# Second and third pair of a fused attention and mixer kernel: ScalarE's root, scaling and rounding queued behind its copies in PSUM, and the remainder rows taken in one visit

## The chip, the cores and the metric

One core of a Trainium2 chip runs the whole kernel. The metric is device time in microseconds (us); the kernel before takes 773.45 us as the median of three runs (773.4 to 773.78). PE is TensorE (matmuls), ACT is ScalarE, DVE is VectorE, POOL is GpSimd, SP is the engine that issues most DMAs. "Bank" below means one of the tiles in PSUM into which PE accumulates.

## The reference, cut to what matters

There are 8 batches of 576 rows, 8 heads of 64 columns, so 512 columns. Attention has no softmax: per head `kv = k^T v`, `out = q kv`, then each row of a head is divided by its root mean square and multiplied with a gain:

```
kv  = einsum('bhsd,bhse->bhde', k, v)
out = einsum('bhsd,bhde->bhse', q, kv)
x   = out / sqrt(mean(out*out, -1) + 1e-6) * g_norm        # (8, 576, 512)
h   = relu(x^T @ w_tok1) @ w_tok2                          # tokens: 576 -> 256 -> 576
u   = x + h^T
out = u + relu(u @ w_ch1) @ w_ch2                          # channels: 512 -> 1536 -> 512
```

All arrays are fp32; the weights arrive as 64-bit floats and are rounded to fp32 on the chip.

## The kernel before, in words

The batches are worked in four pairs (0 to 3). For each pair there is an attention stage (`attention`) that makes x in five tiles X[pair, 0..4] (tiles 0 to 3 hold 2 x 128 rows, tile 4 the 64 remainder rows of both batches), and a token mixing stage (`token_mixing`) that turns x into u. They overlap: while pair p is mixed, the attention of pair p+1 runs. After the fourth pair the channel part begins at about 186 us; it is a long run of block products and isn't touched here.

**An order written out by hand.** Nothing is scheduled by a planner. `play` (L1413) walks through lists of short names (`start`, `middle`, `steady`, `last`, L1474 to L1544) and calls the step of each name; every step's instructions go to their engine in just this order (`keep_in_program_order`), and each engine works its own queue strictly in order. `steady[0]` (L1488) mixes pair 1 beside the attention of pair 2, `steady[1]` (L1493) mixes pair 2 beside pair 3. A leading "-" takes the step from the attention of the pair that is being mixed. The names, with tile c and half or side t:

- `a{c}`: PE's attention products of tile c into two banks; `g`, `q`, `t`: gain on DVE (L495), square on ACT (L499), sum of squares on DVE (L523). `q` of the second bank follows `g` of that bank, and `g` of the first follows `q` of the first: DVE and ACT take turns with a bank.
- `m`, `r`, `i`: mean on DVE (L528), root on ACT (L533), reciprocal with one refinement on DVE (L537 to L542). `s`: ACT scales one half of a tile, head by head (8 instructions, L558). `d`: DVE scales the other half in one instruction (L567). `p21`: POOL does it (L571).
- `kv`, `e`: k^T v on PE and its eviction by ACT. `u{i}`: tok2 of row tile i on PE, with its eviction (a DVE add, L128, or, for the tiles in `seeds`, an ACT copy). `z{i}` (`seed`, L703): ACT copies x into a bank before PE accumulates on it.
- A digit n: the next n steps of `stream` (L1400), the rounding of the channel weights. Block n of 14 has "scale" on ACT (two instructions, L182 and L187, or four, L197 and L200), then "clamp" (L203), "shift" (L207) and "add" (L212, a custom instruction) on DVE. "shift" of block n brings "scale" of block n+1 with it. `f{n}` fetches block n by DMA into one of four staging buffers, which comes free when "add" of block n-4 is done. In all 43 steps; what is left is done in `last`.
- `b`, `l`, `lq`, `lr`: DMAs on SP; `x`: transposes on DVE (L781).

**The seven block products.** For pairs 1 and 2 (`fast`, L599) the first token product is not done row tile by row tile but with seven products of 2x2 blocks. Sums of blocks of w_tok1 are made once by POOL (`mix_tok1`); sums of blocks of x are made per pair by POOL (`t_sum`, names y1 to y4, 128x1024 each). y4 needs X[pair, 3] after both `s30` and `d31`. Four banks are used: a, y, b, d. The order on PE is p1 (a), p5 (b), p6 (y), the attention product a0 of the next pair, p3 (y), p7 (d), p2 (a), then the remainder and p4 (d). Two ACT instructions sit in the chain of PE:

```
        def copied(name, of):          # L656
            h_bank(name)
            copy(bank[name], bank[of])
        def p1():                      # L660
            product("a", a_block(0, 0), x_block(11), True)
            copied("y", "a")
        def p6():                      # L667
            product("y", tok_sum(2), h1[1])
            copied("d", "y")
```

p6 accumulates on the copy "y", so it waits for that copy. p3 overwrites "y", so it waits for the copy "d". p7 copies b and d into h1 (L674), and p4 accumulates on d after that. The remainder rows (64 per batch) are added to y and a in `ha` (`rem_first`, L691) before p4, and to b and d in `hb` (`rem_last`, L697) after it; each is followed by its relus on ACT (L131) and adds on DVE.

Of the kernel before, what the change touches and what calls it, by code (L numbers as in the profile page):

```python
# [20 lines left out]
def kernel(  # L21
# [33 lines left out]
    P = 128  # L55
# [5 lines left out]
    J, JJ, HF, Q = 4, 5, 64, 32  # L61
# [42 lines left out]
    w_tok1r = tokw.tile([P, DTOK], F32, name="w_tok1r")  # L104
# [11 lines left out]
    def do(f, *a, **kw):  # L116
        return lambda: f(*a, **kw)
# [9 lines left out]
    def tensor_add(o, a, b, op=ALU.add, engine=nc.vector):  # L127
        return keep(engine.tensor_tensor(out=o, in0=a, in1=b, op=op))  # L128

    def relu(o, a):  # L130
        keep(nc.scalar.activation(o, a, AF.Relu))  # L131
# [4 lines left out]
    def matmul(*a, **kw):  # L136
        keep(nc.tensor.matmul(*a, **kw))  # L137
# [112 lines left out]
    def get_tok2(t):  # L250
        return block(S, lambda raw: [(raw, words(moe_w_tok2)[ts(t, P)])], w_tok2[:, t])
# [132 lines left out]
    def x_of(pair, i):  # L384

        return X[pair, i // 2][:, i % 2]
# [212 lines left out]
    fast = (1, 2)  # L599
# [11 lines left out]
    def token_mixing(pair, seeds, aside=()):  # L611
        h1, acc = {}, {}
# [19 lines left out]
        bank = {}  # L632
# [49 lines left out]
        def p4():  # L682
            product("d", a_block(1, 1), room)

        def rem(t, names):
            for side in range(2):
                r = ds(side * HF, HF)
                matmul(bank[names[side]], lhsT=w_tok1r[r, ts(t, P)], rhs=x_of(pair, 8)[r],
                       start=False, stop=True, skip_group_check=True)

        def rem_first():  # L691
            rem(0, "ya")
            relu(h1[1][:, 0], bank["a"])
            tensor_add(h1[0][:, 0], bank["y"], h1[0][:, 0])
            relu(h1[0][:, 0], h1[0][:, 0])

        def rem_last():  # L697
            rem(1, "bd")
            relu(h1[1][:, 1], bank["d"])
            tensor_add(h1[0][:, 1], bank["b"], h1[0][:, 1])  # L700
            relu(h1[0][:, 1], h1[0][:, 1])

        def seed(i):  # L703

# [38 lines left out]
        steps = {f"h{s}{t}": do(tok1, s, t) for s in range(2) for t in range(NTOK)}  # L743
# [3 lines left out]
        if pair in fast:  # L747
            steps |= {f"y{n}": do(t_sum, n) for n in range(1, 5)}
            steps |= {"p1": p1, "p2": p2, "p3": p3, "p4": p4, "p5": p5, "p6": p6, "p7": p7}
            steps |= {"ha": rem_first, "hb": rem_last}  # L750
        return steps | {"hr": tok1_rem} | {f"u{i}": do(tok2, i) for i in range(9)}


    xg, xt, uT = {}, {}, {}
# [674 lines left out]
    tok2 = [get_tok2(t) for t in range(NTOK)]  # L1429
# [38 lines left out]
    def spread_g():  # L1468
# [5 lines left out]
    start = [  # L1474
# [12 lines left out]
    steady = [[  # L1487
# [12 lines left out]
    attentions += [attention(p, ((0, 1), (2, 4), (3,))) for p in range(1, B // 2)]  # L1500

    mixings = [token_mixing(p, (2, 3, 4, 5, 6) if p in fast else (2, 4, 6)) for p in range(B // 2 - 1)]
    mixings.append(token_mixing(B // 2 - 1, range(2, 9), (0, 1)))
    more = {f"w{n}{k}": f for n, b in enumerate(first_rows[:1] + tok1[1:] + tok2 + first_rows[1:]) for k, f in enumerate(b)}
    more |= {f"f{n}": b[0] for n, b in enumerate(channel)}
# [139 lines left out]
```

## Time and profile before

| | |
|---|---|
| median of 3 runs | 773.45 us |
| the profiled execution's own time | 773.52 us |
| its span, first to last instruction | 771.5 us |
| PE busy | 760.4 us (99%), clock granted 1.00 |
| DVE busy | 648.5 us (84%) |
| ACT busy | 287.5 us (37%) |
| POOL busy | 130.5 us (17%) |
| mixing of pair 1, from p1 on PE | 71.5 to 114.4 us |
| mixing of pair 2 | 115.4 to 155.0 us |
| token mixing of pair 3 | 154.9 to 186.5 us |
| channel part | 186.5 us to the end |

By stretch of the span, busy us of each engine:

| stretch, us | length | PE | DVE | ACT | POOL |
|---|---|---|---|---|---|
| 78 to 90 | 12 | 10.49 | 10.19 | 8.82 | 2.36 |
| 90 to 102 | 12 | 12.00 | 9.68 | 10.54 | 0.76 |
| 102 to 115 | 13 | 13.00 | 11.35 | 7.82 | 4.95 |
| 115 to 128 | 13 | 11.79 | 9.92 | 8.17 | 8.20 |
| 128 to 140 | 12 | 12.00 | 9.54 | 8.48 | 0.00 |
| 140 to 156 | 16 | 16.00 | 13.99 | 14.94 | 4.27 |
| 156 to 172 | 16 | 16.00 | 15.31 | 9.78 | 1.64 |

A line of the timeline gives the start, the time from there to the end of the last of the merged instructions, engine, source line, operation, output <- inputs, shape and count, and in brackets how long the engine was idle before and what ended that wait. Helpers record operations, so L137 is every matmul and L128 every tensor-tensor; the tile names tell them apart. The views merge buffers of one name: `w_ch` is also where the block sums `room` and `tok_sum` live, `ps_h` is any of the four banks of the seven products.

### The profile page before, as it was taken

Reading aid. Unit: us, or ns where it says so; the run is one execution under the profiler, and the core shown is the slowest. Engines: PE = TensorE matmul, PEld = TensorE weight load, DVE = VectorE, ACT = ScalarE, POOL = GpSimd, SP = SyncE. Lnnn points to the kernel's source line nnn. Section 1 sums busy time; section 2 is a strip of 40 time slices with the busy share of each in tenths; the row PEclk is TensorE's granted clock in tenths of the full one; section 3 lists DMA queues with packets and bytes.
Section 4 is the critical chain, followed back from the end, with each engine's and each line's share of the span. In section 5 each row is a group of like instructions: output and inputs, shape, how many; then the busy total and the mean of one; then the engine's idle time right before and its main releaser. Section 6 shows DMA issues by size and latency. Waiting matters only on the chain.

```text
span 771.5 us, 12763 instructions
## 1 busy us (share of the span) xinstructions
PE 760.4 (99%) x4686; PEld 612.5 (79%) x4686; DVE 648.5 (84%) x960; ACT 287.5 (37%) x579; POOL 130.5 (17%) x134
## 2 busy tenths in 40 slices
PE   9998999999999999999999999999999999999998
PEld 8654454545888888888888888888888888888887
DVE  4868787897776769999978889997998996798996
ACT  3655766864210233521144242223352224325221
POOL 1115133113410000002240001042000218000204
PEclk9999999999999999999999999999999999999999
DMA  9999996797699796599898577999659879855679
GB/s 354 375 370 373 357 353 215 249 365 263 242 283 344 264 291 195 164 270 203 222 231 258 150 221 225 255 185 269 197 152 284 175 220 207 208 145 158 155 192 120
DMA packets 137965, 188.28 MB, mean 244 GB/s; under 512 B 48688, under 2 KB 95792, under 8 KB 135856
## 3 DMA queue, kind: packets, MB, share of 16 engines
q1 hardware_dynamic: 102096, 168.59, 68.2%
q0 software_dynamic: 34848, 18.36, 15.9%
q8 instruction: 38, 0.62, 0.3%
q10 hardware_dynamic: 960, 0.52, 0.2%
q14 instruction: 23, 0.19, 0.1%
HBM read 138.28 MB, written 49.15 MB: 243 GB/s over the span
## 4 chain that ended last, share of the span: by engine, by line
PE 92%; DVE 4%; DMA 2%; ACT 1%; issue 0%; SPq 0%; DVEq 0%; ACTq 0%
PE ps_d L137 28%; PE ps_b L137 19%; PE ps_a L137 19%; PE ps_u L137 7%; PE ps_h L137 6%; PE ps_v L137 5%; PE ps_c L137 3%; PE ps_w L137 2%; PE ps_kv L137 2%; DMA raw<-in_moe_w_tok_dram 1%; PE ps_o L137 1%; DMA v_in<-in_k_dram 1%; DVE x L495 1%; DVE ms L523 1%; DVE w_ch L781 1%; ACT x L558 0%
## 5 line engine op out<-in xcount | busy, mean ns | idle before, releaser
L137 PE MATMUL ps_d<-ui,w 128*128 128x256 f32 x504 | 118.6, 379 | 0.0
L134 ACT COPY ps_d<-ps_a 128x768 f32<-128x768 f32 (+1 forms) x56 | 32.0, 572 | 199.9 <-PE ps_a L137 196.9
L137 PEld LDWEIGHTS ps_d<-ui,w 128*128 128x128 f32 x504 | 95.8, 190 | 13.0
L128 DVE TENSOR_TENSOR v<-v,v 128x1536 f32<-128x1536 f32 (+2 forms) x70 | 103.2, 1482 | 0.3
L137 PE MATMUL ps_b<-sv,w 128*128 128x256 f32 x324 | 78.9, 379 | 0.0
L137 PE MATMUL ps_a<-v,w 128*128 128x256 f32 x324 | 78.7, 379 | 0.0
L1367 POOL DMA_DIRECT2D out_dram<-us x24 | 26.8, 1834 | 291.8 <-ACT p L134 286.5
L137 PEld LDWEIGHTS ps_b<-sv,w 128*128 128x128 f32 x324 | 61.2, 190 | 8.9 <-issue 0.6
L137 PEld LDWEIGHTS ps_a<-v,w 128*128 128x128 f32 x324 | 61.6, 190 | 8.4
L137 PE MATMUL ps_u<-h,w_tok 128*128 128x512 f32 (+1 forms) x160 | 64.7, 599 | 0.0
L131 ACT ACTIVATE v<-v 128x768 f32<-128x768 f32 (+1 forms) x54 | 42.6, 822 | 55.1 <-DVE v L128 55.1
L137 PE MATMUL ps_d<-v,w 128*128 128x256 f32 x258 | 62.7, 379 | 0.0
L1367 POOL DMA_DIRECT2D out_dram<-r x40 | 41.3, 1919 | 102.0 <-ACT p L134 80.3
L137 PE MATMUL ps_d<-sv,w 128*128 128x256 f32 x228 | 55.4, 379 | 0.0
L137 PEld LDWEIGHTS ps_d<-v,w 128*128 128x128 f32 x258 | 48.9, 190 | 6.6
L137 PEld LDWEIGHTS ps_u<-h,w_tok 128*128 128x128 f32 (+1 forms) x160 | 25.6, 179 | 31.1 <-issue 27.0
L137 PEld LDWEIGHTS ps_d<-sv,w 128*128 128x128 f32 x228 | 43.3, 190 | 5.9
L137 PE MATMUL ps_a<-uT,w 128*128 128x256 f32 x192 | 46.7, 379 | 0.0
L137 PE MATMUL ps_b<-ui,w 128*128 128x256 f32 x168 | 40.8, 379 | 0.0
L137 PEld LDWEIGHTS ps_a<-uT,w 128*128 128x128 f32 x192 | 36.5, 190 | 5.0
L128 DVE TENSOR_TENSOR v<-ps_b,u 128x768 f32<-128x768 f32 x28 | 26.8, 956 | 15.6 <-PE ps_b L137 12.5
L134 ACT COPY u<-ps_d 128x256 f32<-128x256 f32 (+1 forms) x44 | 23.2, 528 | 43.4 <-PE ps_d L137 43.4
(198 smaller groups left out, 1358.0 us busy)
## 6 DMA issues: line engine op xcount, KB each, us to landing
w<-parts SPq DMA_DIRECT2D x168, 384.0 KB
w<-parts SPq DMA_DIRECT2D x56, 192.0 KB
uT<-blocks SPq DMA_DIRECT2D x36, 256.0 KB
k_in<-in_k_dram SPq DMA_DIRECT2D x8, 1024.0 KB
v_in<-in_v_dram SPq DMA_DIRECT2D x8, 1024.0 KB
qT<-in_q_dram SPq DMA_DIRECT2D x8, 1024.0 KB
out_dram<-x POOLq DMA_DIRECT2D x16, 512.0 KB, 6.4
raw<-in_moe_w_ch_dram SPq DMA_DIRECT2D x8, 768.0 KB
```

Of the source, the lines that this page charges most:

```text
L128: return keep(engine.tensor_tensor(out=o, in0=a, in1=b, op=op))
L131: keep(nc.scalar.activation(o, a, AF.Relu))
L134: keep(nc.scalar.copy(o, a))
L137: keep(nc.tensor.matmul(*a, **kw))
L495: keep(nc.vector.tensor_mul(x, bank[c, h], g_sb.to_broadcast([P, number(c), D])))
L523: keep(nc.vector.tensor_reduce(stats_of(c)[0][:, h], sq[c, h], axis=AX.X, op=ALU.add))
L781: keep(nc.vector.transpose(y[:, :, o, 2 * i:2 * i + 2].rearrange("p b n t -> p n b t"), x[:, ts(o, DH)].rearrange("p (n b t) -> p n b t", ...
L1367: keep(nc.gpsimd.dma_start(to, t()[ds(b * Q, Q), at].rearrange("p n l j -> p n (l j)"), accum_op=ALU.add))
```

## The change

In both steady lists the steps `r3` (root) and `s30` (scaling of X[pair, 3]) and the first rounding steps move behind the copies into the banks: `r3` from before `p1` to behind it, `s30` and the rounding from beside `p1` and `p5` to behind `p6`. `ha` and `hb` become one step `hr`, placed after `p4`: all the remainder matmuls, on y, a, b and d, then the relus and adds. Rounding steps are dealt out anew: pair 1's list has 15 instead of 14, pair 2's 14 as before, so one fewer is left for `last`.

```
-        def rem(t, names):
-            for side in range(2):
-                r = ds(side * HF, HF)
-                matmul(bank[names[side]], lhsT=w_tok1r[r, ts(t, P)], rhs=x_of(pair, 8)[r],
-                       start=False, stop=True, skip_group_check=True)
-
-        def rem_first():
-            rem(0, "ya")
+        def p_rem():
+            for t, names in enumerate(("ya", "bd")):
+                for side in range(2):
+                    r = ds(side * HF, HF)
+                    matmul(bank[names[side]], lhsT=w_tok1r[r, ts(t, P)], rhs=x_of(pair, 8)[r],
+                           start=False, stop=True, skip_group_check=True)
             relu(h1[1][:, 0], bank["a"])
-            tensor_add(h1[0][:, 0], bank["y"], h1[0][:, 0])
-            relu(h1[0][:, 0], h1[0][:, 0])
-
-        def rem_last():
-            rem(1, "bd")
+            for t, name in enumerate("yb"):
+                tensor_add(h1[0][:, t], bank[name], h1[0][:, t])
+                relu(h1[0][:, t], h1[0][:, t])
             relu(h1[1][:, 1], bank["d"])
-            tensor_add(h1[0][:, 1], bank["b"], h1[0][:, 1])
-            relu(h1[0][:, 1], h1[0][:, 1])
...
     steady = [[
-        "kv00 kv01 e00 e01 -d40 f3", "-u8 y2 y3 -v8 -a3 -q30 -g31 -q31 -g30 -t30 -t31 x01 -m3 -r3 -lq1",
-        "p1 -i3 -d31 -s30 1 l0 b00 1", "p5 1 f4", "p6", "a0 q00 g01 q01 g00 y4", "p3 t00 t01 b01 x10", "p7 1", "p2 1", "ha 1",
-        "p4 1", "hb z2 z3 f5 f6 1", "a1 q10 g11 q11 g10 lq0", "kv10 kv11 e10 e11 t10 t11 m0 r0", "u0 i0 1 1",
-        "u1 z4 d00 s01 l1 1", "u2 z5 1", "a2 q20 g21 q21 g20", "a4 q40 t20 g41 q41 t21 g40 lr0 lr1", "u3 z6 d11",
+        "kv00 kv01 e00 e01 -d40 f3", "-u8 y2 y3 -v8 -a3 -q30 -g31 -q31 -g30 -t30 -t31 x01 -m3 -lq1",
+        "p1 -r3 -i3 -d31 l0 b00", "p5 f4", "p6 -s30 1 1", "a0 q00 g01 q01 g00 y4", "p3 t00 t01 b01 x10", "p7 1", "p2 1 1",
+        "p4 1", "hr z2 z3 f5 f6 1", "a1 q10 g11 q11 g10 lq0", "kv10 kv11 e10 e11 t10 t11 m0 r0 1", "u0 i0 1 1",
+        "u1 z4 d00 s01 l1 1", "u2 z5 1", "a2 q20 g21 q21 g20", "a4 q40 t20 g41 q41 t21 g40 lr0 lr1", "u3 z6 d11 1",
         "u4 s10 t40 t41 m2 r2 f7 1", "u5 i2 1 d20 d21 P2 x11", "u6 f8", "u7 b10 b11"], [
-        "kv00 kv01 e00 e01 -d40 f9", "-u8 y2 y3 -v8 -a3 -q30 -g31 -q31 -g30 -t30 -t31 x20 -m3 -r3 -lq1",
-        "p1 -i3 -d31 -s30", "p5 1", "p6 1", "a0 q00 g01 q01 g00 y4", "p3 t00 t01 x21", "p7 1", "p2 f10", "ha 1", "p4 1", "hb z2 z3 1 1",
+        "kv00 kv01 e00 e01 -d40 f9", "-u8 y2 y3 -v8 -a3 -q30 -g31 -q31 -g30 -t30 -t31 x20 -m3 -lq1",
+        "p1 -r3 -i3 -d31", "p5", "p6 -s30 1 1", "a0 q00 g01 q01 g00 y4", "p3 t00 t01 x21", "p7 1", "p2 f10 1", "p4 1", "hr z2 z3 1 1",
         "a1 q10 g11 q11 g10", "kv10 kv11 e10 e11 t10 t11 m0 r0 b20 b21", "u0 f11 i0 1", "u1 z4 d00 s01 1", "u2 z5",
         "a2 q20 g21 q21 g20", "a4 q40 t20 g41 q41 t21 g40", "u3 z6 d11 1", "u4 s10 t40 t41 m2 r2 1",
         "u5 i2 d20 p21 1", "u6 1 f12", "u7 1", "a3 q30 g31 q31 g30", "u8 v8 t30 t31 m3 r3 f13"]]
```

In the order of instructions on each engine this gives, for ACT around p1 to p7: squares of a3, copy y, root, copy d, eight scalings, one "scale" of the rounding, squares of a0, copies of b and d into h1. After `hr` it gives: relu a, two relus of h1, relu d, seeds z2 and z3, one "scale" of the rounding, squares of a1, the evictions of kv, the root of the next group.

More of the change, by code (lines that the diff above doesn't have):

```diff
@@ L749, in token_mixing @@
             steps |= {"p1": p1, "p2": p2, "p3": p3, "p4": p4, "p5": p5, "p6": p6, "p7": p7}
-            steps |= {"ha": rem_first, "hb": rem_last}
-        return steps | {"hr": tok1_rem} | {f"u{i}": do(tok2, i) for i in range(9)}
+        return steps | {"hr": p_rem if pair in fast else tok1_rem} | {f"u{i}": do(tok2, i) for i in range(9)}
     xg, xt, uT = {}, {}, {}
```

## The prediction

> **What bounds the kernel now.** I read the waits of PE first, then the timelines of PE, ACT, DVE and POOL between 68 and 187 us. PE is busy in 99% of the span, and the waits of PE hold one entry of size after the start (columns: us in total, times, longest):
>
> ```profile
> PE ps_h L137 <- ACT ps_h L134: 4.4, 3, 1.7
> ```
>
> The timeline of PE shows the three places, all in the seven products; the bracket is the idle time. The lines that follow in pair 1 are p2, remainder, p4, remainder; the last is token mixing of pair 3:
>
> ```profile
> 76.93 1.95 PE L137 MATMUL ps_h<-h,w_ch 128*128 128x512 f32 x4 [1.72 <-ACT ps_h L134]
> 78.81 1.16 PE L137 MATMUL ps_o<-kvp,qT 64*64 64x64 f32 x64
> 81.49 1.98 PE L137 MATMUL ps_h<-x,w_ch 128*128 128x512 f32 x4 [1.51 <-ACT ps_h L134]
> ...
> 85.03 1.88 PE L137 MATMUL ps_h<-x,w_tok 128*128 128x512 f32 x4
> 86.83 1.13 PE L137 MATMUL ps_h<-x,w_tok1r 64*128 64x512 f32 x4
> 87.89 1.98 PE L137 MATMUL ps_h<-w_ch,w_tok 128*128 128x512 f32 x4
> 89.81 1.13 PE L137 MATMUL ps_h<-x,w_tok1r 64*128 64x512 f32 x4
> ...
> 120.33 1.96 PE L137 MATMUL ps_h<-h,w_ch 128*128 128x512 f32 x4 [1.21 <-ACT ps_h L134]
> ```
>
> From 186 us on PE waits once, 0.4 us, so what PE has lost or won by then should come through to the end. The question is only what the change does to PE before 186 us.
>
> **What it removes.** A product of four instructions follows another after 1.72 us (83.31 to 85.03). Pair 1: p5 starts at 73.33, so p6 could start at 75.05 instead of 76.93: 1.88 us. "y" can be copied as soon as p1 ends (73.50), and p6's other operand, y2 on POOL, is ready at 73.70. p3 could follow a0 after 1.09 (78.02; "d" copied from 77.03 to 77.61) instead of after 2.68: 1.59. Pair 2: p6 at 118.96 instead of 120.33: 1.37. The remainder in one visit: p2 to the end of the second remainder takes 90.87 - 85.03 = 5.84; p2 1.72, p4 1.82 and eight remainder instructions 1.92 (row at 42.35, to 44.27) make 5.46: 0.38 per pair. Sum 1.88 + 1.59 + 1.37 + 0.76 = 5.60 us. That would be the change if nothing else were late.
>
> **What comes late next, pair 1.** Here are the rows of POOL and DVE that decide it: y4, and the "add" of block 0.
>
> ```profile
> 79.48 2.36 POOL L128 TENSOR_TENSOR w_ch<-x,h 128x1024 f32<-128x1024 f32 x1 [1.89 <-ACT x L558]
> ```
> ```profile
> 80.19 2.46 DVE L212 CUSTOM_DVE_ANT_1 w_ch<-w_ch,raw 128x1536 uint16<-128x1536 uint16 x1 [1.71 <-ACT w_ch L182]
> ...
> 93.88 0.69 DVE L495 TENSOR_TENSOR x<-ps_o,g_sb 128x512 f32<-128x512 f32 x1 [0.75 <-ACT sq L499]
> ```
>
> The add waits for "scale" of block 1 (L182), takes 2.46 us where the next ones take 0.96, and ends 0.81 after POOL's y4: DVE stands while POOL works. After the change copy d sits before s30, so s30 runs from 77.55 to E = 79.57 (2.02, as now), y4 to 82.08, add to 82.89, g01 starts at 82.93. ACT's second square follows g01 after 0.78 (83.17 to 83.95 now): 83.71; then copies of b and d to 85.30. p4 must wait for that copy, and p4 is no longer behind a remainder but right after p2. PE, gaining 3.47, wants it at 83.28 and gets it at about 85.4: a new stall of 2.1.
>
> [...]
>
> Next, the queues behind `hr`. DVE goes g01, g00, two sums, four transposes, clamp, shift, add, clamp, then the add of y: 82.93 + 3.72 (83.17 to 86.89 now) + 0.58 + 0.55 + 0.88 + 0.48 = 89.14. Relus of h1 end at 91.1, relu d and the seeds z2 and z3 at 92.6. Now "scale" of block 3 stands before the squares of a1, which it did not: two instructions of 0.80. The first square starts at 94.16; it starts now in this line:
>
> ```profile
> 92.23 1.09 ACT L134 COPY ps_u<-x 128x512 f32<-128x512 f32 x2
> 93.26 1.07 ACT L499 ACTIVATE sq<-ps_o 128x512 f32<-128x512 f32 x2
> ...
> 104.76 0.61 ACT L134 COPY ps_u<-x 128x512 f32<-128x512 f32 x1
> ```
>
> So 0.90 later. DVE waits for it (g10, 93.88 now) for 3.3 us instead of 0.75, then has the "add" of block 2 (0.88) ahead of the eviction of u0, less a wait that goes: g21 of a2 at 102.92 (101.72 now, +1.20). ACT's squares of a2 and a4 follow DVE, and behind them is seed z6 (the last line above): 105.96 to 106.57 instead of 104.76. u6 on PE accumulates on z6. Now it starts at 106.51 and z6 is 1.1 ahead. After the change PE is there at 104.8 (85.4, p4 1.82, remainder 1.92, a1 1.09, kv 2.48, u0 to u2 5.35, a2 0.98, a4 0.58, three u of 1.72) and waits to 106.65. **Pair 1 gives +0.15: its gain is spent twice.**
>
> **Pair 2.** Behind z6 "scale" of block 5 (1.6) now stands ahead of s10 and root 2: the reciprocals come at 110.72 (107.93 now), the scaling of X[2, 2] ends at 113.48 (111.01), and POOL's y1, y2, y3 end at 116.04, 119.17 and 121.53 (113.57, 116.91, 119.23). PE needs y1 at 117.4 and y2 at 119.1: p6 at 119.25, a gain of 1.08. The mean m3 is one of the DVE forms that stand while POOL works (75.45, 0.60, ending with y3, where 119.31 took 0.13), so it ends at 121.55; root, copy d (122.27; p3 wants 122.22), s30 to E = 124.86, y4 to 127.37. "add" of block 5 needs no scale and is through before y4. ACT then has scale 6, two squares and the copies of b and d: 128.45; p4 wants 127.64 and starts at 128.55. `hr` ends at 132.29, 0.39 ahead of 132.68. Then again: relus to 133.98, relu d, z2 and z3 to 135.55, "scale" of block 8 of four instructions (2.42) ahead of the squares: 137.97 instead of 135.15. DVE stands 3.5 us. z6 ends at 148.66; u6, now at 148.32, wants 147.95 and starts at 148.75: **+0.43**.
>
> **Pair 3.** DVE is full there (15.31 of 16 us) and starts later: "scale" of block 9 and s10 ahead of root 2 bring the reciprocals to 153.65 (150.27), "add" of block 9 (1.13) has moved ahead of a3's gain, which comes at 158.85 (155.71). s30 of pair 3 ends at 165.4; now:
>
> ```profile
> 160.54 2.02 ACT L558 ACTIVATE x<-x,inv 128x64 f32<-128x64 f32 x8 [1.03 <-DVE inv L542]
> ```
> ```profile
> 154.90 14.00 PE L137 MATMUL ps_h<-x,w_tok 128*128 128x512 f32 x32
> ```
>
> Of these 32 instructions the 21st is the first to read it, at 154.90 + 20 x 0.43 = 163.5, 0.95 after it is ready. After the change PE is there at 163.95 and waits to 165.45: **+1.9 in all**. The remainder tile (d40, 166.6) is in time for 170.8. The sums on DVE end some 3 us later than now, at about 184 for PE's use at 188: hidden. DMA: block 9's fetch and the qT behind it on SP, issued at 129.49 and 130.42 now, come earlier, since "add" of block 5 is earlier; f6 and what stands behind it come 5 us later, for use 30 us on: nothing either way.
>
> **Sum.** 773.52 + 1.9 = 775.4 us against the profiled execution's own time; that one is 0.07 above the median, which is less than the rounding here.
>
> **Bounds.** From ACT's end to PE is 0.06 to 0.15. The add behind y4: 0.81 to 0.96. What the walk can miss most is the two waits of DVE for the squares (3.3 and 3.5 against 0.75 and 0.17 now). If each is shorter by 1, u6 costs nothing in either pair, p6 gains, and pair 3 does not wait: 773.0 or a little below. If DVE is 2 us later still in pair 3, its wait grows by as much: 777.4.
>
> **Rivals.**
> - **The later waits are not there; one stall is left** (faster). If rounding behind `hr` does not hold the squares, z6 comes in time, and pair 1 keeps 3.85 less the 2.1 at p4 = 1.75, pair 2 keeps 0.39 to 1.75: 773.52 - 2.1 to 3.5, about 770.8. For it: ACT is busy only 8.8 of 12 us there. Against: it is order, not load; the scale stands ahead of the squares in the queue. It decides where z6 in pair 1 ends before 105.
> - **All of it is won**: 773.52 - 5.60 = 767.9. For it: each of the three waits is PE's own, with PE on the chain before and after. Against: p4's wait needs y4 and the add to be over 2 us sooner than the rows allow.
> - **The change does not reach the time**: the gains are spent at p4 and u6 and pair 3 just escapes: 773.4 to 774.5. This differs from the forecast in one margin, s30 against PE in pair 3.
> - **DVE's backlog grows**: more waits in pair 3 or at the start of the channel part, 777 to 779. Against: channel sums have 4 us in hand.
>
> **How the numbers follow.** Forecast 0.42; not reached 0.26; one stall left 0.18; all won 0.06; backlog 0.08. What a measurement of this kernel can tell is about 0.2%, 1.55 us: 771.9 to 775.0. The forecast lies just above that, so a third of it counts as within: faster 0.23, within 0.38, slower 0.39. The range 770.2 to 778.0 leaves out the all-won case and the far ends.
>
> **What would show it.** Right: no wait for the copies "y" and "d" at p6 and p3; a wait of about 2 at p4 of pair 1 for ACT's copy into h1; a wait at the seventh tok2 product (u6) in one or both pairs; DVE idle over 2.5 us at g10 waiting for ACT's square; a wait in pair 3's tok1 for L558. Wrong: if u6 starts before 105.5 in pair 1, the queue behind `hr` was not what I take it for; if pair 3's tok1 runs through, 1.5 us fall away.

## The result, and the profile after

The changed kernel takes 776.76 us (median of 7 runs, 775.57 to 776.91), the kernel before on the same chip 773.55 (773.4 to 774.44). The ratio is 1.0035, with a 95% interval of 1.0023 to 1.0046: slower by about a third of a percent, which is 2.7 us by the ratio and 3.2 between the medians. The profiled execution took 776.9, with a span of 775.0. PE was idle for 11.1 us in the span before and for 13.6 in the one after.

The waits of PE after (us in total, times, longest) have three new entries behind 68 us, and the 4.4 us for the copies in PSUM are gone:

```profile
PE ps_h L137 <- ACT h L134: 3.6, 2, 2.8
PE ps_u L137 <- ACT ps_u L134: 1.8, 2, 1.0
PE ps_h L137 <- ACT x L558: 1.8, 1, 1.8
```

The timeline of PE after shows where. These are p6, a0 and p3 of pair 1, p2, p4 and the remainder; then u6 of pair 1, p6 of pair 2, its p4 and u6, and token mixing of pair 3:

```profile
73.86 1.98 PE L137 MATMUL ps_h<-h,w_ch 128*128 128x512 f32 x4
75.77 1.16 PE L137 MATMUL ps_o<-kvp,qT 64*64 64x64 f32 x64
76.93 1.98 PE L137 MATMUL ps_h<-x,w_ch 128*128 128x512 f32 x4
...
80.47 1.88 PE L137 MATMUL ps_h<-x,w_tok 128*128 128x512 f32 x4
85.16 2.83 PE L137 MATMUL ps_h<-w_ch,w_tok 128*128 128x512 f32 x4 [2.82 <-ACT h L134]
87.92 2.76 PE L137 MATMUL ps_h<-x,w_tok1r 64*128 64x512 f32 x8
...
107.53 3.70 PE L137 MATMUL ps_u<-h,w_tok 128*128 128x512 f32 x8 [1.02 <-ACT ps_u L134]
...
120.01 1.98 PE L137 MATMUL ps_h<-h,w_ch 128*128 128x512 f32 x4
...
129.27 1.96 PE L137 MATMUL ps_h<-w_ch,w_tok 128*128 128x512 f32 x4 [0.77 <-ACT h L134]
...
149.79 3.70 PE L137 MATMUL ps_u<-h,w_tok 128*128 128x512 f32 x8 [0.83 <-ACT ps_u L134]
...
167.05 5.42 PE L137 MATMUL ps_h<-x,w_tok 128*128 128x512 f32 x12 [1.81 <-ACT x L558]
```

p6 and p3 run straight through, as they should: three brackets of the profile before are gone. In their place there are five others, of 7.25 us in all. And one thing has no bracket: the four instructions of p4 took 2.83 to their end and the eight of the remainder 2.76, where the same shapes take 1.9 and 2.0 elsewhere. The busy time by stretch has the reason in its column PEclk, the third from the right, which is the granted clock, 1.00 at full speed (here the rows from 82 to 93 us; the columns are the stretch, its length, the busy us of PE, its weight loads, DVE, ACT and POOL, then PEclk, the DMA engines' busy share and GB/s):

```profile
82.00:85.20 3.20, 0.38 (x2) 0.07 (x1) 3.20 (x6) 1.75 (x4) 0.00 (x0) 1.00 1.02 418
85.20:87.90 2.70, 2.70 (x4) 0.74 (x4) 2.63 (x7) 1.43 (x2) 0.00 (x0) 0.67 1.07 370
87.90:90.60 2.70, 2.70 (x9) 1.03 (x8) 1.75 (x3) 0.60 (x1) 0.00 (x0) 0.70 1.05 364
90.60:93.00 2.40, 2.40 (x110) 2.32 (x110) 1.86 (x4) 2.19 (x5) 0.00 (x0) 1.00 0.89 292
```

Behind the stall the clock averages 0.67 and 0.70 over two rows. Rows of 0.1 us show that these are averages: the clock is 1.00 until 86.1, 0.50 from there to 89.5, and 1.00 again behind that. Half a clock for 3.4 us is 1.7 us of work lost.

The stall itself goes back to y4 and the "add" of block 0, which runs beside it as before; the gains of a0 come behind it, and through ACT's second square the copies of b and d:

```profile
79.58 2.37 POOL L128 TENSOR_TENSOR w_ch<-x,h 128x1024 f32<-128x1024 f32 x1 [1.86 <-ACT x L558]
```
```profile
80.28 2.48 DVE L212 CUSTOM_DVE_ANT_1 w_ch<-w_ch,raw 128x1536 uint16<-128x1536 uint16 x1 [1.70 <-ACT w_ch L182]
```

The queues behind `hr` read as forecast. On ACT and DVE after, the first square of a1, DVE's wait for it at g10, and seed z6:

```profile
95.09 1.06 ACT L499 ACTIVATE sq<-ps_o 128x512 f32<-128x512 f32 x2
...
106.87 0.61 ACT L134 COPY ps_u<-x 128x512 f32<-128x512 f32 x1
```
```profile
95.70 0.69 DVE L495 TENSOR_TENSOR x<-ps_o,g_sb 128x512 f32<-128x512 f32 x1 [3.15 <-ACT sq L499]
...
139.32 0.69 DVE L495 TENSOR_TENSOR x<-ps_o,g_sb 128x512 f32<-128x512 f32 x1 [3.42 <-ACT sq L499]
```

DVE stood 3.15 us in pair 1 and 3.42 in pair 2 for a square that stands behind a "scale" of the rounding; before it stood 0.75 and 0.17. The second of these is, before:

```profile
135.77 0.69 DVE L495 TENSOR_TENSOR x<-ps_o,g_sb 128x512 f32<-128x512 f32 x1 [0.17 <-ACT sq L499]
```

In pair 3 the scaling of X[3, 3] ran from 164.97 to 166.99 (160.54 to 162.56 before), and PE went on at 167.05. The channel part begins at 190.11 instead of 186.55: these 3.56 us are the loss, and behind that point nothing changes (the span is 3.5 longer). Its first line before, and after:

```profile
186.55 1.99 PE L137 MATMUL ps_v<-uT,w_ch 128*128 128x256 f32 x8
```
```profile
190.11 1.99 PE L137 MATMUL ps_v<-uT,w_ch 128*128 128x256 f32 x8
```

### The profile page after: what moved, and what is told of

Its sections match the earlier page's. It is cut to its first block, busy times and chain, and to the rows that moved or that the text cites. A ratio compares the mean times of both kernels' runs of the same rounds, so it can differ in the third digit from the quotient of the medians.

```text
span 775.0 us, 12764 instructions
## 1 busy us (share of the span) xinstructions
PE 761.4 (98%) x4686; PEld 611.8 (79%) x4686; DVE 648.5 (84%) x960; ACT 287.2 (37%) x579; POOL 131.5 (17%) x134
## 4 chain that ended last, share of the span: by engine, by line
PE 84%; DVE 7%; ACT 4%; DMA 2%; issue 2%; SPq 0%; DVEq 0%; ACTq 0%
PE ps_d L137 28%; PE ps_b L137 19%; PE ps_a L137 19%; PE ps_v L137 5%; PE ps_u L137 4%; PE ps_h L137 3%; PE ps_c L137 3%; PE ps_w L137 2%; ACT x L558 2%; DMA raw<-in_moe_w_tok_dram 1%; DVE ms L523 1%; DVE x L495 1%; PE ps_kv L137 1%; DMA v_in<-in_k_dram 1%; DVE x L567 1%
## 5 line engine op out<-in xcount | busy, mean ns | idle before, releaser
L137 PE MATMUL ps_h<-x,w_tok 128*128 128x512 f32 x80 | 37.1, 604 | 2.5 <-ACT x L558 1.8
```

## The experiments

**The theory**: moving the copies ahead is good by itself; the loss comes (1) from "scale" ahead of the squares of a1, behind `hr`, (2) from the add of block 0 that runs beside y4 and holds back p4, and (3) from the one rounding step more in pair 1, which shifts the stream, so that scales and adds stand ahead of squares, root and gain in pairs 2 and 3. **The rival**: the moved work is simply too much for DVE and ACT there, and any order of it ends in a wait. A second question is the clock: does it fall because PE stood still?

### Scale, gain, or both in another place; the copies alone

The first four were run together, beside the kernel before at 773.58 us (27 runs). Later groups ran on other chips; the kernel before took 773.51 to 773.65 us beside each of them, so that times are compared across groups here. The changed kernel was not run again beside them: its 776.76 is the one given above.

e1_scale_ahead_of_hr, both pairs:

```diff
-  "p4 1", "hr z2 z3 f5 f6 1", ...            "p4 1", "hr z2 z3 1 1",
+  "p4 1 1", "hr z2 z3 f5 f6", ...            "p4 1 1 1", "hr z2 z3",
```

> The changed kernel, with only the scale of the rounding that stood between the seeds and the squares of a1 moved ahead of the remainder (pair 1: one step, pair 2: two). If the queue behind the remainder is what costs (my theory), the square of a1 starts about 1.6 us sooner in pair 1 and 2 sooner in pair 2, DVE's wait for it falls below 2, neither u6 nor pair 3's tok1 waits (1.0, 0.8 and 1.8 less), while p4's wait of 2.8 in pair 1 and the lower clock behind it stay: 772.3 to 773.8 us. If the cost is the scaling of X[pair, 3] behind copy d and the stall at p4 with the clock that falls there (the rival), it stays at 775.5 to 777.

774.08 us (773.46 to 774.93), ratio 1.0004 [0.9995, 1.0014]: faster than the changed kernel, but a little above the 772.3 to 773.8 that the theory gave. The squares of a1 start at 92.69 instead of 95.09, u6 of pair 1 waits 0.44 instead of 1.02, and u6 of pair 2 not at all. p4 (2.81) still waits, as expected; tok1 of pair 3 (1.70) waits too, where the theory had it gone. So (1) is worth 2.7 us between the medians; in executions at a clock of 1.00 (below) it is 775.6 - 773.5 = 2.1.

e2_gain_ahead_of_add, pair 1:

```diff
-  "p6 -s30 1 1", "a0 q00 g01 q01 g00 y4",
+  "p6 -s30 1", "a0 q00 g01 q01 g00 y4 1",
```

> The changed kernel, with only the add of block 0 in pair 1 moved behind the gains of a0. If DVE's standing behind POOL's y4 makes p4 late, g01 starts near 78.7, the copy of d ends near 83 and p4's wait falls from 2.8 to about 0.9 us; the granted clock stays 1.00, so p4 and remainder take 3.7 instead of 5.5. The rival (stall and clock are the cost) then expects about 773 us or less. My theory expects the larger part of it to be lost again at u6, which waits for seed z6: 774 to 775.5, with u6's wait grown above 1 us in pair 1.

775.02 us (774.7 to 775.58), ratio 1.0017 [1.0008, 1.0026], within the theory's range. The timeline of PE in this kernel, p4 and u6 of pair 1:

```profile
83.08 1.96 PE L137 MATMUL ps_h<-w_ch,w_tok 128*128 128x512 f32 x4 [0.74 <-ACT h L134]
...
105.42 5.40 PE L137 MATMUL ps_u<-h,w_tok 128*128 128x512 f32 x8 [2.12 <-ACT ps_u L134]
```

p4's stall falls from 2.82 to 0.74, so all but this much of it was the add behind y4. But PE then comes to u6 earlier than the seed z6 and waits 2.12 there, and now these eight instructions take 5.40 instead of 3.70: the low clock has moved along with the longest stall. PE leaves the remainder 3.7 us ahead of the changed kernel (86.89 instead of 90.61: the shorter stall and the full clock) and leaves u6 only 0.4 ahead (110.75 instead of 111.16). In pair 2 p4 no longer waits (0.77 in the changed kernel), and from u6 of pair 2 on PE is 1.6 ahead, which is the 1.7 between the medians.

e3_both (the edits of e1_scale_ahead_of_hr and e2_gain_ahead_of_add):

> Both of the above. My theory: the waits at p4, u6 and pair 3's tok1 are all cut, 770 to 772 us, faster than the kernel before. The rival expects no more than the second alone brings, 773.

772.67 us (772.58 to 772.86), ratio 0.9984 [0.9975, 0.9993]; the theory's 770 to 772 is missed. p4 waits 0.75 in both pairs, u6 of pair 1 1.65, tok1 of pair 3 1.73. The two edits are worth 4.1 us between the medians, but not what the removal should bring; the wait in pair 3 is untouched by either.

e5_copies_alone: the kernel before, with the root behind copy "y" and scaling and rounding behind copy "d"; the remainder stays in two visits, the steps are 14 in pair 1:

```diff
-  ... x01 -m3 -r3 -lq1", "p1 -i3 -d31 -s30 1 l0 b00 1", "p5 1 f4", "p6",
+  ... x01 -m3 -lq1",     "p1 -r3 -i3 -d31 l0 b00",      "p5 f4",   "p6 -s30 1 1 1",
...
-  ... x20 -m3 -r3 -lq1", "p1 -i3 -d31 -s30", "p5 1", "p6 1",
+  ... x20 -m3 -lq1",     "p1 -r3 -i3 -d31",  "p5",   "p6 -s30 1 1",
```

> The kernel before, with only root, scaling and first rounding behind the copies; the remainder stays in two visits around p4, the rounding elsewhere as it was. My theory: the three waits for the copies go, p4 stands a remainder (1.06) later and waits less than 1.5 us, the scale ahead of the squares is not there, so u6 hardly waits: 770.5 to 772.5 us. The rival (the moved scaling is harmful by itself) expects 774 or more.

771.7 us (770.68 to 771.86), ratio 0.9967 [0.9955, 0.998]: faster. This half of the change, by itself, gains. PE has one wait of size left, at p4, longer than the 1.5 us that the theory allowed, and again with a low clock behind it (p4 2.67 to its end instead of 1.9):

```profile
86.01 2.67 PE L137 MATMUL ps_h<-w_ch,w_tok 128*128 128x512 f32 x4 [2.34 <-ACT h L134]
```

No wait at u6, none in pair 3. So the three waits of the copies can be had without the two late ones.

### One step less, the remainder alone, and the parts put together

The next four were run together, beside the kernel before at 773.51 us (21 runs).

e8_one_step_less: the changed kernel, one digit taken out of pair 1.

```diff
-  "u3 z6 d11 1",
+  "u3 z6 d11",
```

> The changed kernel with one rounding step taken out of pair 1 (the one behind u3, so that it is taken later), nothing else. Theory (the step too many is what shifts the stream, puts the scales of blocks 8 and 9 ahead of squares and root, and the add of block 9 ahead of the gain of a3): p4's 2.8 and u6's 1.0 in pair 1 stay, u6 of pair 2 and L558 of pair 3 no longer wait (0.8 and 1.8): 773.5 to 774.8. Rival (pair 2 and 3 are late because pair 1 was, or because of the one visit): waits as in the changed kernel, 775.5 to 777.

772.55 us (771.47 to 774.13), ratio 0.9985 [0.9976, 0.9994]. One digit is worth 4.2 us between the medians. p4 (2.61) and u6 of pair 1 (1.02) wait as in the changed kernel; all the waits of pairs 2 and 3 are gone, that of p4 in pair 2 among them. The first square of a1 in pair 2 comes at 135.02 (138.72 in the changed kernel), the scaling of X[3, 3] at 160.43 (164.97; 160.54 before):

```profile
135.02 1.08 ACT L499 ACTIVATE sq<-ps_o 128x512 f32<-128x512 f32 x2
...
160.43 2.02 ACT L558 ACTIVATE x<-x,inv 128x64 f32<-128x64 f32 x8 [1.03 <-DVE inv L542]
```

It went below what either theory gave: by its brackets the three waits are 3.4 us, by the starts of the instructions 4.2 (190.11 to 185.89 at the channel part), and the 0.77 at p4 of pair 2 had not been counted. This settles (3): what the forecast had as "scale of block 5", "of block 8" and "add of block 9" ahead of their neighbours is one step too many, and not the late pair 1, which is as late here (u6 starts at 107.64, and at 107.53 in the changed kernel).

e4_remainder_alone: the changed kernel's single visit with the copies, root, scaling and rounding where they were (the edit is against the kernel before).

```diff
-  "p7 1", "p2 1", "ha 1", "p4 1", "hb z2 z3 f5 f6 1",
+  "p7 1", "p2 1 1", "p4 1", "hr z2 z3 f5 f6 1",
...
-  "p7 1", "p2 f10", "ha 1", "p4 1", "hb z2 z3 1 1",
+  "p7 1", "p2 f10 1", "p4 1", "hr z2 z3 1 1",
```

> The other half of the change alone: the remainder of both token tiles in one visit of PE, with the copies y and d, the root and the scaling in the order of before, and as many rounding steps in pair 1 as before (14). Theory (the visit in one is cheap, the loss comes from the extra rounding step and from the stall at p4): p4 wants PE at about 86.7 and its copy is there at 85.5, so no wait at p4; the rounding steps have the phase of before, so no scale stands ahead of the squares of a1, no wait over 0.5 at u6, none at L558 in pair 3. The waits of 1.7, 1.5 and 1.2 for the copies stay. Time 772.5 to 773.6. Rival (the one visit itself throws VectorE back, because both additions and four relus now come behind the last product): VectorE waits over 2.5 us for the first square of a1 here too, u6 or tok1 of pair 3 waits over 1 us: 774.5 to 776.

772.99 us (772.68 to 773.92), ratio 0.9992 [0.9983, 1.0001]: 0.5 us, within what can be told from no change. p4 does not wait, nor u6, nor pair 3; VectorE waits 1.24 and 0.65 for the first squares, not over 2.5. The single visit is harmless; whether its 0.38 per pair is there, the time alone cannot tell. In this profile PE came to p6 1.0 us earlier than in the one of before and waited 3.11 for copy "y"; p4 is at 87.11.

e6_copies_gain_ahead: e5_copies_alone with the gain of a0 ahead of the add.

```diff
-  "p6 -s30 1 1 1", "a0 q00 g01 q01 g00 y4",
+  "p6 -s30 1", "a0 q00 g01 q01 g00 y4 1 1",
```

> The copies moved alone, with the remainder in two visits as before, and in pair 1 the gain of a0 ahead of the rounding's add. Theory (the 2.34 us at p4 and the low clock behind it are what was left of the loss in the kernel with the copies alone, and they come from the add behind y4): p4's wait is under 0.3, the granted clock stays at 1.00 from 80 to 95 us, and the time falls from 771.7 to 768.5 to 770. Rival (VectorE's work is only put off, and PE waits for it at u6 or in tok1 of pair 3 by about as much): 771 to 772.

769.85 us (769.62 to 770.14), ratio 0.9951 [0.9939, 0.9964]. p4 runs through and the clock is 1.00. Two waits come in its place, 0.45 at u0 for a relu and 1.08 at u6 for seed z6: the rival is there too, with 1.5 of the 2.3 us. That the time still falls by 1.9 about fits: 2.34 of waiting and 1.7 of slow clock go, 1.5 of waiting come, which makes 2.5; by the start of the channel part in the two profiles it is 2.2 (182.75 instead of 184.95).

e7_all_phase_of_before: the changed kernel with the gain ahead of the add and 14 steps in pair 1.

```diff
-  "p6 -s30 1 1", "a0 q00 g01 q01 g00 y4", ... "kv10 ... m0 r0 1", ... "u3 z6 d11 1",
+  "p6 -s30 1", "a0 q00 g01 q01 g00 y4 1 1", ... "kv10 ... m0 r0", ... "u3 z6 d11",
```

> The whole change, with the gain of a0 ahead of the add and with 14 rounding steps in pair 1 instead of 15, so that from pair 2 on the stream of steps stands as it did before. Theory: p4 waits 0.7 as in the kernel with the gain ahead, the two scales no longer stand ahead of the squares, u6 waits under 0.7 in pair 1 and not in pair 2, L558 not at all: 768.5 to 770.5, that is 2 to 4 below the kernel with scale and gain both moved (772.67). Rival (the phase does not matter, the load of VectorE does): u6 and L558 wait 1.6 and 1.7 as there, 772 to 773.

769.03 us (768.89 to 769.06), ratio 0.994 [0.9926, 0.9954]: the best version, 7.7 us below the changed kernel with the same instructions; only u6's wait is above the 0.7 that was expected. All that PE waits for between 68 and 186 us:

```profile
82.96 1.96 PE L137 MATMUL ps_h<-w_ch,w_tok 128*128 128x512 f32 x4 [0.74 <-ACT h L134]
103.54 3.70 PE L137 MATMUL ps_u<-h,w_tok 128*128 128x512 f32 x8 [0.88 <-ACT ps_u L134]
```

The rival "any order ends in a wait of the same size" has fallen. Of the 5.60 us that the removal was worth in the forecast, 4.5 are here.

e10_seed_earlier: e7_all_phase_of_before with the seed z6 of pair 1 ahead of the squares of a2. (Run with e9_no_idle_at_p4, beside 773.52, 9 runs.)

```diff
-  "u2 z5 1", ... "u3 z6 d11",
+  "u2 z5 z6 1", ... "u3 d11",
```

> The kernel with the whole change, the gain ahead and the phase of before (769.03), with the seed z6 of pair 1 put ahead of the squares of a2. Theory (u6's wait of 0.88 is only the seed behind the squares in ScalarE's queue): u6 of pair 1 does not wait, 768.2 to 768.7. Rival (the seed's bank comes free late or VectorE's gain of a2, 0.6 later, makes the evictions late): a wait of 0.5 or more at u5 to u7, 768.9 to 769.8.

769.12 us (768.71 to 769.42), ratio 0.994 [0.9927, 0.9952]: nothing gained over 769.03, though u6 does not wait any more. PE has a new wait of 0.75 at p4 of pair 2 instead. Neither theory had the place: the 0.88 at u6 go, and nearly as much is waited one pair later.

### Does PE's clock fall because PE stands still?

e9_no_idle_at_p4: the changed kernel with six products that nobody reads between p2 and p4 of pair 1.

```diff
+    def warm():
+        o = ps["kv"].tile([P, DM], F32, name="ps_w", tag="kv")
+        for _ in range(6):
+            matmul(o, lhsT=ones, rhs=w_tok2[:, 0, :DM], start=True, stop=True)
+
+    more["jw"] = warm
...
-  "p7 1", "p2 1 1",
+  "p7 1", "p2 1 1 jw",
```

> The changed kernel with six products of 128x512 that nobody reads between p2 and p4 of pair 1 (6 x 0.43 = 2.6 us by the rows of tok2), so that TensorE is busy through the stall of 2.8; p4 still starts when its copy is there. Theory (the missed 1.7 us are the granted clock, which falls because TensorE stood still): p4's wait is under 0.5, p4 starts at 85.2 as in the changed kernel, the clock stays at 1.00 from 85 to 91 us, p4 and the remainder take 1.8 and 1.9, and the times, which lay at 775.6 with a mean clock of 1.000 and at 776.9 with 0.998, all lie at 775.3 to 775.8. Rival (the clock falls for another reason in that stretch, such as what the other engines draw): the clock falls here too, in most executions, and the median stays at 776.5 to 777.

779.41 us (779.25 to 779.62), ratio 1.0073 [1.006, 1.0087]. The size was wrong: each product is two instructions, so the six took 5.2 us and not 2.6, and they waited 1.75 for a square of ACT before they began; p4 started at 89.31 instead of 85.16. As a measurement of the question it says one thing: with PE idle for 1.75 at a stretch, and then busy, the clock stayed at 1.00, and the mean clock was 0.999 or 1.000 in all five executions. p4 and the remainder took 1.88 and 1.99.

e11_idle_cut_short and e12_one_step_less_idle_cut: one such product instead of six, in the changed kernel and in e8_one_step_less (beside 773.65, 15 runs).

> The changed kernel with one product of 128x512 that nobody reads between p2 and p4 of pair 1: two instructions, 0.86 us by the rows of e9_no_idle_at_p4, where they started at 84.06. They end at about 84.95, ahead of 85.16, where p4 of the changed kernel gets its copy: p4 should start at the same time as there, but TensorE stands 1.75 us at a stretch instead of 2.82. Theory (the clock falls because TensorE stands too long): the clock stays at 1.00 from 85 to 91 us in every execution (mean 0.999 or 1.000), p4 and the remainder take 1.9 and 2.0 instead of 2.76 and 2.69, and the times lie at 775.3 to 776.0, all together. Rival (the clock falls for another reason in that stretch): most executions at 0.998 and 776.7 to 777, as in the changed kernel.

775.73 us (775.42 to 776.9), ratio 1.0027 [1.0016, 1.0039].

> The kernel with one step less in pair 1 (e8_one_step_less: times at 771.5, 772.6 and 774.0 with mean clocks of 1.000, 0.998 and 0.995), with the same one product between p2 and p4. Theory: all executions at 771.3 to 772.0, clock 0.999 or more. Rival: the levels of 772.6 and 774.0 are still there.

771.59 us (771.35 to 772.96), ratio 0.9976 [0.9967, 0.9986].

The executions sort by their mean granted clock. Times in us:

| kernel | PE idle at a stretch at p4 | clock 0.999 or 1.000 | clock 0.998 or less |
|---|---|---|---|
| changed | 2.82 | 3 of 7: 775.57 to 775.83 | 4: 776.76 to 776.91 |
| changed, e11_idle_cut_short | 1.75 | 5 of 7: 775.42 to 775.75 | 2: 776.73, 776.9 |
| e8_one_step_less | 2.61 | 3 of 11: 771.47 to 771.64 | 6: 772.5 to 772.82; 2 at 0.995: 773.98, 774.13 |
| e12_one_step_less_idle_cut | 1.76 | 7 of 9: 771.35 to 771.74 | 2: 772.85, 772.96 |
| e1_scale_ahead_of_hr | 2.81 | 3 of 11: 773.46 to 773.57 | 8: 773.88 to 774.93 |
| e2_gain_ahead_of_add | 0.74 (2.12 at u6) | 5 of 11: 774.7 to 774.94 | 6: 775.02 to 775.58 |
| e5_copies_alone | 2.34 | 2 of 5: 770.68, 770.84 | 3: 771.7 to 771.86 |
| e3_both, e7_all_phase_of_before | 0.75, 0.74 (1.65, 0.88 at u6) | 16 of 16 | none |

The mean does not say where in an execution the clock fell; only a profile does, and each kernel has one. In the changed kernel, e8, e11 and e12 an execution with a low clock is 1.0 to 1.4 us longer between the medians (2.5 at 0.995), in e1, e2 and e5 0.5 to 1.1. With the idle time cut to 1.75 it comes in 4 of 16 executions instead of 12 of 18, p4 itself starting as before. So it is rarer behind the shorter stall, as the theory says; but it did not go away, as the theory said. The profile of e11_idle_cut_short is one in which it came, that of e12_one_step_less_idle_cut one in which it did not; the lines are the extra product and p4 of pair 1:

```profile
83.98 1.13 PE L137 MATMUL ps_w<-w_tok,ones 128*128 128x512 f32 x2 [1.75 <-ACT sq L499]
85.04 3.65 PE L137 MATMUL ps_h<-w_ch,w_tok 128*128 128x512 f32 x4
```
```profile
84.11 1.12 PE L137 MATMUL ps_w<-w_tok,ones 128*128 128x512 f32 x2 [1.76 <-ACT sq L499]
85.16 1.96 PE L137 MATMUL ps_h<-w_ch,w_tok 128*128 128x512 f32 x4
```

The same instructions after the same wait take 3.65 us in the one and 1.96 in the other. What decides between the two executions stays open.

The two executions also give the price of a fall. e12_one_step_less_idle_cut and e8_one_step_less have the same pair 1 up to u6 but for the one product; p4 starts at 85.16 and 85.27. Without a fall the squares of a1 start at 93.84 and u6 at 106.26 after a wait of 1.40; with one, at 95.21 and 107.64 after 1.02. So of the 1.7 us that PE loses, some 0.4 are taken up by a shorter wait at u6, and 1.4 are left.

## Why the prediction was right, and where its size was off

The forecast was 775.4 us and the result 776.76. Its mechanism held step by step: every sign that it named as right is in the profile. One term was mis-sized, the work behind the new stall.

- **The removed waits.** p6 and p3 of pair 1 and p6 of pair 2 wait for no copy. e5_copies_alone shows that this is worth something: 1.9 us net of a new 2.3 us stall, and 3.7 with that stall gone (e6_copies_gain_ahead), of the 4.84 (1.88 + 1.59 + 1.37) that the forecast had for the copies.
- **p4 of pair 1.** Forecast: start at 85.4 after a wait of 2.1. Measured: 85.16 after 2.82; PE was there 0.9 earlier (p1 at 70.20 and not 71.51, since 1.1 us of idle time ahead of it, at ps_r with no releaser, is in the profile of before and not in this one). That is not the change: in the profiles of the experiments, two of them built on the kernel before, this idle time is at most 0.25 us. It made the stall longer and left p4's start where it was, since the copies of b and d set it, as the forecast said. The row of the add was right: it ended at 82.76, 0.81 behind y4 as before; the 0.96 at the upper end of the forecast's bounds is in neither profile.
- **The term that was mis-sized.** p4 and the remainder were priced at 1.82 and 1.92, from rows at a clock of 1.00. They took 2.76 (85.16 to 87.92) and 2.69 (87.92 to 90.61): 1.71 us more, with the clock at 0.50 for 3.4 us. The step that failed is the price of work *behind* a new stall. In the three executions with the clock at 1.000 or 0.999 the time was 775.57 to 775.83, 0.2 to 0.4 from the forecast.
- **The queue behind `hr`.** Forecast from p4's start on: squares of a1 at 94.16, DVE idle 3.3, z6 at 105.96, u6 of pair 1 at 106.65. Measured: 95.09, 3.15, 106.87 and 107.53, so the starts are some 0.9 later. Without a fall of the clock they are 0.3 to 0.4 earlier than forecast (93.84, 105.60 and 106.26 in e12_one_step_less_idle_cut, DVE idle 3.21), so the walk was right here and the clock is the difference. e1_scale_ahead_of_hr shows that the scale's place is the cause of the queue: the squares come 2.4 earlier there.
- **Pair 2.** y1 to y3 end at 116.87, 119.95 and 122.27 (forecast 116.04, 119.17, 121.53), p6 at 120.01 (119.25), p4 at 129.27 (128.55), DVE idle 3.42 (3.5), u6 at 149.79 (148.75): the same shape, 0.7 to 1.0 later.
- **Pair 3.** Forecast a wait of 1.5 for the scaling, to 165.45; measured 1.81, to 167.05. This is 1.6 later, where u6 of pair 2 was 1.0 later: some 0.5 were added on DVE, between the reciprocals (154.75, forecast 153.65) and the gain of a3 (160.40, forecast 158.85). The forecast gave pair 2 and 3 as the places where the gain is lost, to blocks 5, 8 and 9 standing one place further ahead. e8_one_step_less confirms this as one cause, and prices it at 4.2 us: one digit in one list.
- **The rivals.** "One stall left", 770.8, needs z6 of pair 1 to end before 105; it ended at 107.48. The 8.8 of 12 us that spoke for it are those of 78 to 90 us; behind the remainder, from 90 to 102, ACT was busy for 10.54 of 12. It is not this kernel; e7_all_phase_of_before and e6_copies_gain_ahead are near what it described, with the order changed. "DVE's backlog grows" was right in the small: pair 3's wait was 0.3 longer, and no new one came behind it.

## What to carry to other kernels

In a kernel whose order is written by hand, a step added early in a shared stream (here one rounding step of 14) shifts every later one by a place; look two stages on for what now stands ahead of a square, a root or a gain. An instruction moved out of the path of one wait has to be followed to the next place where PE meets the same queue: p4, u6 and pair 3 each took back a part here. And in this kernel the price of a stall of 1.75 us or more on PE was its length and, in many executions, 1.7 us of slower work behind it, less what a following wait took up (0.4 at u6).

## What the runs showed of the hardware

The granted clock of PE fell at stalls of 3.11 us (e4_remainder_alone), 2.82 (the changed kernel), 2.61 (e8_one_step_less), 2.34 (e5_copies_alone), 2.12 (e2_gain_ahead_of_add: eight instructions in 5.40 us instead of 3.70) and, in some executions, of 1.75 (e11_idle_cut_short). In the changed kernel rows of 0.1 us show 0.50 for 3.4 us (86.1 to 89.5); in e11_idle_cut_short the row from 85.2 to 87.9 has 0.50. The other rows are longer than the fall or hold a part of it, and their means are:

| kernel | mean granted clock |
|---|---|
| e4_remainder_alone | 0.62 (76 to 79), 0.81 (79 to 82) |
| e8_one_step_less | 0.62 (85 to 88), 0.81 (88 to 91) |
| e5_copies_alone | 0.85 (85 to 88), 0.58 (88 to 91) |
| e2_gain_ahead_of_add | 0.77 (104 to 108), 0.81 (108 to 112) |
| e11_idle_cut_short | 0.99 (82 to 85.2), 0.50 (85.2 to 87.9), 0.88 (87.9 to 90.6) |

One fall to 0.50 of 3.4 us gives these means in all five, whatever the length of the stall. Worked out from them, it begins 2.5 to 3.8 us after PE began to stand: in e4_remainder_alone still within the stall (76.7, PE stood from 74.19 to 77.30), in the others 0.4 to 1.1 us after PE had started again. So the price was the same each time, 1.7 us of PE's work where all of the fall lay behind the stall. The clock did not fall at every such stall: the profile of e1_scale_ahead_of_hr has a stall of 2.81 and 1.00 behind it.

```profile
85.01 1.95 PE L137 MATMUL ps_h<-w_ch,w_tok 128*128 128x512 f32 x4 [2.81 <-ACT h L134]
```

In the kernel before, a mean clock of 0.996 to 0.998 cost nothing that the times show: of the 72 executions beside the experiments 40 have it and 21 have 1.000, and both lie at 773.3 to 774.1 us (ten at 0.995 at 774.7 to 775.0). That another wait soon follows there and takes up the difference is argued, from one trace: in e4_remainder_alone p6 ran for 3.36 us at a low clock, behind 3.11 of waiting, and p3, which waited 1.51 in the kernel before, then did not wait at all. The one profile of the kernel before has no fall, so where its clock falls in the other executions is not shown.
